# Mixer products in 128x64 halves among a convolution's last step

## The chip, the cores and the metric

The kernel runs on one core of one Trainium2 chip. A core has TensorE (matrix products, with a separate path that loads the stationary operand), VectorE (DVE in the profile), ScalarE (ACT), GpSimd (POOL) and SyncE (SP, which here issues most DMAs). TensorE multiplies a stationary tile of up to 128 rows by 128 columns with a moving operand and writes into PSUM, which has 8 banks; ScalarE and VectorE read the banks and write to the on-chip memory. The metric is the device time of one execution in microseconds; the median of three runs of the kernel before is 226.26 us (226.03 to 226.96).

## The reference

Two branches work on the same input `x = A_q` (2048 tokens, 640 channels) and are mixed by a gate per token:

```python
g = _sigmoid((x * gate_w).sum(-1, keepdims=True))
return g * a + (1 - g) * b
```

Branch `a` is a long convolution. The key is shifted by a short filter of four taps and multiplied with the value (`kv`); `kv` is convolved over the 2048 tokens with a kernel of the same length per channel, by an FFT of 4096; the result is multiplied by the query. Branch `b` is a Mixer block:

```python
h = _gelu(_layernorm(x) @ w1)                 # 640 -> 640
hs = concat(four channel groups of h, shifted by 1, -1, 2, -2 tokens) @ w2
x1 = x + hs
h2 = _gelu(_layernorm(x1) @ w3) @ w4          # 640 -> 1536 -> 640
return x1 + h2
```

## The kernel before

Everything is written as a list of 778 tasks (`build`). A task has an engine, a function that issues its instructions, the tasks it depends on, and the buffers it takes and gives back. The order of all tasks is a string of numbers written out by hand (`ORDER`); a letter behind a number chooses the engine where there are two. `place` walks through that order once with a model of the times and picks for every task its buffer numbers: above all the PSUM banks (`U`). Its model adds `SWITCH` (0.096) to a TensorE task whose `mode` differs from that of the task before, so the label `mode` can influence which bank a task gets; it changes no instruction by itself. Then every engine's instructions are issued in that order, and the framework adds the waits.

The 2048 tokens are 16 blocks of 128 (`s`), four blocks make a quarter (`c`). The Mixer's second half does this for each quarter: layer norm and a transpose by DMA give `x1nT`; twelve tasks `w3.c.fb` (line 810 on) each multiply five tiles of W3 with the quarter's 512 tokens into one bank, five matmuls of 128x128 with 512 columns; ScalarE takes the GELU of each bank (line 820) into `h2T`. Then for each block a task `w4.s` (line 827) multiplies twelve tiles of `h2T` with W4, 512 columns and then 128 columns, 24 matmuls in two banks, and VectorE adds the result to `x` (line 842). For blocks 12 to 15 (`LATE`) w4 is two tasks of twelve matmuls, `w4.s.0` with 512 columns and `w4.s.1` with 128 (line 834), each in a bank of its own.

The convolution is four steps of small products around transfers through DRAM. Steps 1 to 3 use tiles of 64 and 32 rows. Step 4 (line 1023) makes the output of one block: a product with 64 stationary columns for each half of the output partitions, with 512 and with 128 columns of the moving operand. So a task `s4.s` has four matmuls on 128x64 tiles: the two halves of 512 columns, then the two of 128. It needs a load of `GX` from DRAM. VectorE then multiplies its two banks with the gate and the query (`yq`, line 1029; the query arrives by a DMA into `QO`, two buffers for pairs of blocks), and adds the Mixer's part (`ad`, line 1056, or for blocks 12 to 15 `ax`, line 1037, and after w4 `fo`, line 1043). The output is stored by SyncE, for blocks 12 to 15 by SyncE and ScalarE.

In the last part of the order TensorE's tasks stand like this (`s4` is the convolution's last step, the rest the Mixer's):

```
... w4.9 w4.6 | s4.6 s4.7 | w3.3.0 w3.3.6 | s4.2 s4.3 | w3.3.1 w3.3.3 | s4.4 s4.5 s4.1 | w4.8 w3.3.4 w3.3.11 |
s4.0 s4.9 s4.8 | w3.3.7 w3.3.5 w3.3.8 w3.3.2 w3.3.9 | s4.15 | w3.3.10 | s4.10 s4.14 s4.11 | w4.13.0 w4.12.0 |
s4.12 s4.13 | w4.13.1 w4.14.0 w4.12.1 w4.14.1 w4.15.0 w4.15.1
```

A bar marks a change between 128x128 and 128x64 tiles. VectorE's order in the same stretch puts `yq` of blocks 15 and 14 with their `ax`, then `ad` and `yq` of blocks 0, 1, 11, 10, 13, 12, and last the eight `fo` of blocks 12 to 15, of which block 15's two end the work.

Of the kernel before, what the change touches and what calls it, by code (L numbers as in the profile page):

```python
# [16 lines left out]
P = 128  # L17
# [17 lines left out]


ORDER = """
41 0 23 5 29 94v 6 7 9 3 19 11 17 4 25 1 2 31 32 15 18 8 10 63v 12 13 14 26 27 87v 61a 85a 64 62 95v 104v 65v 28
42 88 86 393 24 44 96 209 43 210 55a 66v 89v 67 395 56 68a 58a 53v 54 97v 34 90a 30 399 396v 400v 57v 91 397 40
394a 93a 98 59 99v 100v 92v 60v 101 103v 143 147 16 20p 33 149 398a 102a 77a 145 79v 21 45 150 80 391 71v 72 46  # L40
22 144 148 69v 392v 82v 74a 121 39 122 450 70 78 146 107a 73v 458 35 75 451v 401p 438 37 81v 76v 439a 151 83
113v 123 36 459a 38 456 152 457a 49 84v 108 114 454 452 115v 116 125 455a 453a 110v 129 117v 446 444 126 460
118v 403 404 405 124 127 447a 162 163 406 130 128 156 157 440 105a 441a 407 159 153 154 106 160 461 47 445a 402
131 158 109a 155 442 111 132 137 443a 112a 408 161 462 466 48 138 409 463a 448 134 135 468 215p 216 449 164 140
469a 467a 119 413 141 51 221p 165 470 410 50 411 120a 166 222 223v 464 465a 167 474 471a 173 475a 174 171 217a
480 168 476 187 191 481a 482 193 477a 172 473 192 188 412 414 218 483a 478 169 195 189 170 181 415 416 417 479a
472 418 419 421 422 182 178 179 485 196 194 190 486 423 488 219a 484 225a 489a 175 220 487a 492 176 493a 136 203
424 204 494 425 490 206 498 207 495a 200 201 491a 420 426 427 428 430 502 499a 226 177 504 224 505a 211 503a 506
500 227 496 501a 239 507a 133 497 228 240 508 142 429 184 185 139 247 431 432 433 434 435 436 248 233 510 512
511a 231 513a 243 259p 509 249 514 235 234 260 232 244 515a 518 245 265p 250 236 229 52 519a 516 437 212 246  # L50
517a 520 241 242 237 230 522 266 261v 523v 526 238 530 527a 197 524 531a 528 255 521 529a 269v 262 525v 186 694v
263a 180 205 208 532 267v 303v 198 253 251 257 256 533 183 268 309v 353v 213 202 310 254 270 252 304 313a 264
307v 199 311v 534 535 537 271 539 258 536v 305a 538a 354 540 541v 272 571 566 542 555 293 544 543a 545 572 294
574 575a 289 567 569 570v 573a 550 290 277 598 556 558 278 568v 291 551 557a 292 552a 306 559v 553 546 554a 547a
279 280 283 576 577 284 548v 603 604 606 607a 599 587 287 635 312 273 600a 288 560 561 562 274 285 564a 605v 601
355v 308 286 563v 588 589a 590 591a 602v 582 275 276 578 314 614 580a 619 608 583 609 347p 348 579a 315 325 316
667 584v 549 585 357v 586a 214 615 617 335 616v 620 326 622 336 623a 592 618a 317 323 318 324 621v 593 610 611a
630 612v 333 636 334 631 633 329 349v 662 319 637v 624 634a 646 706 632a 625 594 281 330 320 647 595a 596v 648v
724 638 282 651 649 581 351v 321 565 652 597 639a 654 350 653a 650v 655a 331 626 322 656 657 628a 295 640 641
668 332 670 627a 669a 337 613 678 338 296 642 671v 643v 644a 683 658 663 352 660a 664a 327 328 358 665 659v 679  # L60
695 666a 356 672 673 681 343 684 661 682a 680a 685a 344 674 686 687a 688 629 297 645 675a 689 676v 690 677 301
692v 691a 693 345 302 341 298 299 723 725 346 342 300 696 728 359 371 705 707 729 710 714 360 372 361 365 362
# [4 lines left out]
"""  # L67
ENGINE = {"a": "ACT", "v": "DVE", "p": "POOL"}

# [286 lines left out]
def build(env, nc, io):  # L356
# [6 lines left out]
    ONE = ("U", 1, False)  # L363
# [50 lines left out]
    def c_ones(t):  # L414
# [6 lines left out]
        w=[("K", "z")], roles=("K",))  # L421

    def c_warm(t):
# [4 lines left out]
        r=["WA"], w=["WB"])  # L428
# [354 lines left out]
    def f_st2(t, s0):  # L783
# [3 lines left out]
        nc.gpsimd.tensor_tensor(out=nb, in0=r, in1=SS("S1")[:, c], op=ALU.mult)  # L787
        nc.gpsimd.tensor_scalar(out=nb, in0=nb, scalar1=-1.0 / D, scalar2=None, op0=ALU.mult)

    LATE, late = (12, 13, 14, 15), {}  # L790
    for c in range(4):
        nT, nP = None, f"x1nT{c % 2}"
        for s0 in (4 * c, 4 * c + 2):
            ss = (s0, s0 + 1)
            add(f"ve2.{s0}", {"DVE": 0.42, "POOL": 1.5}, 0, lambda t, s0=s0: f_ve2(t, s0), r=[("x", s, 0) for s in ss] + [("S2", s) for s in ss],
                w=[("v2", s0)])
            add(f"st2.{s0}", "POOL", 1.5, lambda t, s0=s0: f_st2(t, s0), r=[("v2", s0)] + [("x", s, 0) for s in ss],
                w=[("r2", s) for s in ss])
            for s in ss:
                def f_nm2(t, s=s):  # L800
                    k = slice(s, s + 1)
                    norm(t, env["xn"][:, t.buf["xn"][0], :], env["x"][:, s, :], SS("r2")[:, k], SS("SB")[:, k])
                n = add(f"nm2.{s}", {"DVE": 0.445, "ACT": 0.93}, 0, f_nm2, r=[("r2", s), ("x", s, 0)], acq=("xn",))
                def f_dt(t, s=s, n=n, nP=nP):
                    nc.sync.dma_start_transpose(out=env.nT(int(nP[-1]))[:, s % 4, :, :], in_=env["xn"][:, n.buf["xn"][0], :])
                tt = add(f"dt2.{s}", "SP", 1.25, f_dt, use=[n] + ([nT] if nT else []), rel=[(n, "xn")], nbytes=P * D * BF * 1.8,
                         acq=() if nT else (nP,), w=[("x1nT", s)], after=("hsT",) if c % 2 else ())
                nT = nT or tt
        h2 = None
        for fb in range(12):  # L810
            def w3(t, fb=fb, nP=nP):
                for kb in range(5):
                    nc.tensor.matmul(env.PS[:, t.buf["U"][0], :], lhsT=env["W3"][:, kb, 128 * fb:128 * fb + 128],  # L813
                                     rhs=env.nT(int(nP[-1]))[:, :, kb, :], start=(kb == 0), stop=(kb == 4))
            t = add(f"w3.{c}.{fb}", "PE", 1.09, w3, r=["W3"] + [("x1nT", 4 * c + i) for i in range(4)], rel=[(nT, nP)],
                    use=[h2] if h2 else [], acq=[ONE] if h2 else [ONE, "h2"], after=("xnT",), mode="f")
            h2 = h2 or t

            def g2(t_, fb=fb, t=t, o=h2):
                nc.scalar.activation(out=env["h2T"][:, o.buf["h2"][0], fb, :], in_=env.PS[:, t.buf["U"][0], :], func=ACT.Gelu_apprx_tanh)  # L820
            add(f"g2.{c}.{fb}", "ACT", 0.61, g2, use=[t], rel=[(t, "U")], w=[("h2", c, fb)])
        for s in range(4 * c, 4 * c + 4):
            def w4(t, s=s, o=h2):
                m = env.Uf(t.buf["U"][0])
                for (c0, c1) in ((0, 512), (512, 640)):
                    for fb in range(12):
                        nc.tensor.matmul(m[:, c0:c1], lhsT=env["h2T"][:, o.buf["h2"][0], fb, 128 * (s % 4):128 * (s % 4) + 128],  # L827
                                         rhs=env["W4"][:, fb, c0:c1], start=(fb == 0), stop=(fb == 11))
            kw = dict(r=["W4"] + [("h2", c, fb) for fb in range(12)], rel=[(h2, "h2")], mode="f")
            if s in LATE:  # L830
                for n, (c0, c1) in enumerate(((0, 512), (512, 640))):
                    def w4n(t, c0=c0, c1=c1, s=s, o=h2):
                        for fb in range(12):
                            nc.tensor.matmul(env.PS[:, t.buf["U"][0], 0:c1 - c0], lhsT=env["h2T"][:, o.buf["h2"][0], fb, 128 * (s % 4):128 * (s % 4) + 128],  # L834
                                             rhs=env["W4"][:, fb, c0:c1], start=(fb == 0), stop=(fb == 11))
                    late[s, n] = add(f"w4.{s}.{n}", "PE", (2.62, 0.68)[n], w4n, acq=[ONE], **kw)
                continue
            t = add(f"w4.{s}", "PE", 3.28, w4, acq=("U",), **kw)

            def t2(t_, s=s, t=t):  # L840
                x = env["x"][:, s, :]
                nc.vector.tensor_tensor(out=x, in0=env.Uf(t.buf["U"][0])[:, 0:D], in1=x, op=ALU.add)  # L842
            add(f"t2.{s}", "DVE", 0.83, t2, use=[t], rel=[(t, "U")], w=[("x", s, 0), ("x", s, 1)])
# [255 lines left out]
```

## Time and profile before

| | |
|---|---|
| median of three runs | 226.26 us |
| profiled execution, first to last instruction | 225.3 us |
| TensorE busy | 214.4 us (95%) |
| VectorE busy | 188.8 us (84%) |
| ScalarE busy | 154.7 us (69%) |
| GpSimd busy | 45.9 us (20%) |

The profile gives the profiled execution's span from first to last instruction, 225.3 us; the time of a run also holds what lies around it, and the median is 0.96 us above the span. In the views, PE is TensorE, PEld its weight loads, which overlap its matmuls; L followed by a number is a line of the kernel; a name such as `PS<-W,h2T` gives the tile that an instruction writes and those that it reads; `128*64` is the size of the stationary tile, `128x512` that of the moving operand. In the chain of waits, each row is a piece of the chain of work that ended last: when the piece begins, how long it is, and whose work it is. Records of some matmuls can be missing, and matmuls overlap each other's ends, so the start to start distance tells more than a record's length.

### The profile page before, as it was taken

How to read it: one execution, taken by the hardware profiler on the slowest of the kernel's cores; microseconds unless marked ns; L12 is line 12 of the kernel's file. 1: busy time of each engine (PE TensorE's matmuls, PEld its weight loads, DVE VectorE, ACT ScalarE, POOL GpSimd, SP SyncE). 2: the span in 40 equal slices, each digit the busy share in tenths (PEclk: the TensorE clock that was granted, in tenths of full speed). 3: DMA queues.
4: the chain of work that ended last, by engine and by line, in shares of the span. 5: the costliest groups of instructions: out<-in, count | busy, mean ns of one | idle time of the engine just before them, and what ended most of it. 6: DMA issues, size and time to landing. Idle time of an engine off the chain costs nothing.

```text
span 225.3 us, 5017 instructions
## 1 busy us (share of the span) xinstructions
PE 214.4 (95%) x1978; PEld 104.2 (46%) x1998; DVE 188.8 (84%) x281; ACT 154.7 (69%) x225; POOL 45.9 (20%) x86
## 2 busy tenths in 40 slices
PE   3999999999999999999999999999999999999993
PEld 1576454556444444345543333334445554544462
DVE  7898897999999999997479989899767327988993
ACT  6988999699988999789568988878875002125000
POOL 7373451446100009920800000000000000000000
PEclk9999999999999999999999999999999999999998
DMA  6999998999999969979999969999982596888524
GB/s 194 274 335 244 238 245 255 292 225 355 322 210 368 205 231 298 378 254 246 237 390 311 305 190 288 279 323 340 221 269 87 160 414 188 256 268 249 166 58 116
DMA packets 39501, 57.90 MB, mean 257 GB/s; under 512 B 15027, under 2 KB 30645, under 8 KB 39478
## 3 DMA queue, kind: packets, MB, share of 16 engines
q1 hardware_dynamic: 39158, 57.27, 88.9%
q10 hardware_dynamic: 320, 0.33, 0.5%
q8 instruction: 15, 0.25, 0.4%
q14 instruction: 8, 0.07, 0.1%
HBM read 35.56 MB, written 18.36 MB: 239 GB/s over the span
## 4 chain that ended last, share of the span: by engine, by line
PE 72%; DVE 11%; DMA 9%; ACT 4%; issue 2%; POOL 1%; DVEq 0%; POOLq 0%
PE PS L813 18%; PE PS L827 17%; PE PS L716 9%; DMA C<-TRIG 7%; PE PS L834 6%; PE PS L957 5%; PE PS L690 4%; PE PS L985 4%; DVE VC L870 3%; DVE VC L874 3%; PE PS L1023 2%; DMA K<-in_A_k_dram 2%; ACT FS L388 2%; PE PS L256 2%; PE PS L903 2%
## 5 line engine op out<-in xcount | busy, mean ns | idle before, releaser
L820 ACT ACTIVATE h2T<-PS 128x512 bf16<-128x512 f32 x48 | 27.9, 605 | 28.4 <-PE PS L813 28.0
L827 PE MATMUL PS<-W,h2T 128*128 128x128 bf16 (+1 forms) x281 | 39.8, 297 | 0.4
L388 ACT CAST FS<-PS 128x1024 bf16<-128x1024 f32 x37 | 36.0, 1019 | 5.6 <-PE PS L905 3.5
L813 PEld LDWEIGHTS <-W 128*128 128x128 bf16 x240 | 21.1, 98 | 30.7 <-issue 9.4
L827 PEld LDWEIGHTS <-h2T 128*128 128x128 bf16 x288 | 22.2, 98 | 18.9 <-issue 1.9
L388 ACT CAST XH<-PS 128x1024 bf16<-128x1024 f32 x26 | 25.5, 1020 | 7.5 <-PE PS L957 7.4
L813 PE MATMUL PS<-x1nT,W 128*128 128x512 bf16 x120 | 28.5, 380 | 0.0
L813 PE MATMUL PS<-XB,W 128*128 128x512 bf16 x120 | 28.5, 380 | 0.0
L972 DVE TENSOR_TENSOR PP<-XH 128x2048 bf16<-128x2048 bf16 x20 | 23.7, 1220 | 3.1 <-ACT XH L388 2.8
L870 DVE TENSOR_TENSOR VC<-K,VC 128x2560 bf16<-128x2560 bf16 x16 | 23.7, 1491 | 1.7 <-DMA W<-in_B_w_dram 1.5
L716 PE MATMUL PS<-W,hsT 128*128 128x128 bf16 (+1 forms) x155 | 23.5, 297 | 1.0 <-ACT hsT L707 0.7
L842 DVE TENSOR_TENSOR x<-PS,x 128x640 bf16<-128x640 f32 x12 | 9.8, 824 | 13.7 <-PE PS L827 13.7
L690 PE MATMUL PS<-xnT,W 128*128 128x512 bf16 x80 | 19.2, 379 | 0.1
L716 PEld LDWEIGHTS <-hsT 128*128 128x128 bf16 x160 | 12.8, 98 | 13.1 <-DMA W<-in_B_w_dram 1.2
L874 DVE TENSOR_TENSOR VC<-VC 128x2560 bf16<-128x2560 bf16 x12 | 17.9, 1491 | 0.3
L390 DVE CAST XH<-PS 128x1024 bf16<-128x1024 f32 x14 | 16.9, 1220 | 1.2 <-PE PS L957 1.1
L1029 DVE SCALAR_TENSOR_TENSOR W<-PS,GG,QO 128x640 bf16<-128x640 f32 x16 | 13.6, 879 | 2.5 <-PE PS L1023 2.2
L388 ACT CAST GS<-PS 128x1024 bf16<-128x1024 f32 x12 | 12.0, 1016 | 3.9 <-PE PS L985 3.9
L256 PE MATMUL PS<-C 128*128 128x512 bf16 x34 | 10.7, 460 | 3.8 <-DVE C L507 3.7
L834 PE MATMUL PS<-W,h2T 128*128 128x128 bf16 (+1 forms) x94 | 13.3, 298 | 0.1
L723 DVE SCALAR_TENSOR_TENSOR x<-PS,x 128x640 bf16<-128x640 f32 x16 | 12.9, 820 | 0.3 <-PE PS L716 0.3
L957 PE MATMUL PS<-FX,TRIG 64*32 64x512 bf16 x320 | 12.4, 381 | 0.3 <-ACT GS L388 0.3
(115 smaller groups left out, 292.5 us busy)
## 6 DMA issues: line engine op xcount, KB each, us to landing
FH<-FS SPq DMA_DIRECT2D x8, 640.0 KB, 5.3
FXD<-FS SPq DMA_DIRECT2D x8, 640.0 KB, 5.4
FX<-FH SPq DMA_DIRECT2D x10, 512.0 KB, 5.8
FX<-FXD SPq DMA_DIRECT2D x10, 512.0 KB, 5.3
GX<-GD SPq DMA_DIRECT2D x8, 640.0 KB, 5.9
W<-in_B_w_dram SPq DMA_DIRECT2D x2, 1920.0 KB, 11.9
GD<-GS SPq DMA_DIRECT2D x8, 480.0 KB, 4.4
SK<-in_A_ssm_k_dram SPq DMA_DIRECT2D x5, 512.0 KB, 6.8
```

Of the source, the lines that this page charges most:

```text
L388: nc.scalar.copy(out=out, in_=in_)
L390: (nc.vector if t.on == "DVE" else nc.gpsimd).tensor_copy(out=out, in_=in_)
L690: nc.tensor.matmul(m[:, b, :], lhsT=W[:, 0, kb, 160 * fb:160 * fb + 128], rhs=rhs(kb, shifts[fb]), start=(kb == 0), stop=(kb == 4))
L716: nc.tensor.matmul(m[:, c0:c1], lhsT=env["hsT"][:, o.buf["hs"][0], fb, 128 * (s % 4):128 * (s % 4) + 128], rhs=env["W12"][:, 1, fb, c0:c1] ...
L813: nc.tensor.matmul(env.PS[:, t.buf["U"][0], :], lhsT=env["W3"][:, kb, 128 * fb:128 * fb + 128], rhs=env.nT(int(nP[-1]))[:, :, kb, :], star ...
L820: nc.scalar.activation(out=env["h2T"][:, o.buf["h2"][0], fb, :], in_=env.PS[:, t.buf["U"][0], :], func=ACT.Gelu_apprx_tanh)
L827: nc.tensor.matmul(m[:, c0:c1], lhsT=env["h2T"][:, o.buf["h2"][0], fb, 128 * (s % 4):128 * (s % 4) + 128], rhs=env["W4"][:, fb, c0:c1], st ...
L834: nc.tensor.matmul(env.PS[:, t.buf["U"][0], 0:c1 - c0], lhsT=env["h2T"][:, o.buf["h2"][0], fb, 128 * (s % 4):128 * (s % 4) + 128], rhs=env ...
L870: nc.vector.tensor_tensor(out=VC[:, o], in0=env["K"][:, a + 3 - j:a + 7 - j, :], in1=w, op=ALU.mult)
L874: nc.vector.tensor_tensor(out=VC[:, 1], in0=VC[:, 1], in1=VC[:, 2], op=ALU.add)
L957: nc.tensor.matmul(env.U(t.buf["U"][0])[32 * j:32 * j + 32, gp, :], lhsT=CRI()[64 * gp:64 * gp + 64, 32 * pc:32 * pc + 32], rhs=X[64 * gp: ...
L972: nc.vector.tensor_tensor(out=env["PP"][:, o.buf["PP"][0], a, :].rearrange("p (b c) -> p b c", b=2), in0=X.unsqueeze(1).broadcast_to([P, 2 ...
```

## The change

The Mixer's products from the first step-4 task on are issued as pairs: instead of one matmul with a stationary tile of 128x128, two with 128x64, one for each half of the output partitions. Both halves read the same moving operand, and the second follows the first at once. This holds for w3 of the last quarter (`c == 3`), for w4 of block 8 and for w4 of blocks 12 to 15, whose tasks get the mode `c64` that the step-4 tasks have. The numbers in `ORDER` are the same, only broken into other lines.

```diff
+    def halves_of(t):
+        return ((0, 64), (64, 64)) if t.mode == "c64" else ((0, P),)
+
     LATE, late = (12, 13, 14, 15), {}
+    COLS = (8, 12, 13, 14, 15)
...
             def w3(t, fb=fb, nP=nP):
                 for kb in range(5):
-                    nc.tensor.matmul(env.PS[:, t.buf["U"][0], :], lhsT=env["W3"][:, kb, 128 * fb:128 * fb + 128],
-                                     rhs=env.nT(int(nP[-1]))[:, :, kb, :], start=(kb == 0), stop=(kb == 4))
+                    for q, w in halves_of(t):
+                        nc.tensor.matmul(env.PS[q:q + w, t.buf["U"][0], :], lhsT=env["W3"][:, kb, 128 * fb + q:128 * fb + q + w],
+                                         rhs=env.nT(int(nP[-1]))[:, :, kb, :], start=(kb == 0), stop=(kb == 4))
             t = add(f"w3.{c}.{fb}", "PE", 1.09, w3, r=["W3"] + [("x1nT", 4 * c + i) for i in range(4)], rel=[(nT, nP)],
-                    use=[h2] if h2 else [], acq=[ONE] if h2 else [ONE, "h2"], after=("xnT",), mode="f")
+                    use=[h2] if h2 else [], acq=[ONE] if h2 else [ONE, "h2"], after=("xnT",), mode="c64" if c == 3 else "f")
...
                 for (c0, c1) in ((0, 512), (512, 640)):
                     for fb in range(12):
-                        nc.tensor.matmul(m[:, c0:c1], lhsT=env["h2T"][:, o.buf["h2"][0], fb, 128 * (s % 4):128 * (s % 4) + 128],
-                                         rhs=env["W4"][:, fb, c0:c1], start=(fb == 0), stop=(fb == 11))
-            kw = dict(r=["W4"] + [("h2", c, fb) for fb in range(12)], rel=[(h2, "h2")], mode="f")
+                        for q, w in halves_of(t):
+                            a = 128 * (s % 4) + q
+                            nc.tensor.matmul(m[q:q + w, c0:c1], lhsT=env["h2T"][:, o.buf["h2"][0], fb, a:a + w],
+                                             rhs=env["W4"][:, fb, c0:c1], start=(fb == 0), stop=(fb == 11))
+            kw = dict(r=["W4"] + [("h2", c, fb) for fb in range(12)], rel=[(h2, "h2")], mode="c64" if s in COLS else "f")
             if s in LATE:
...
                         for fb in range(12):
-                            nc.tensor.matmul(env.PS[:, t.buf["U"][0], 0:c1 - c0], lhsT=env["h2T"][:, o.buf["h2"][0], fb, 128 * (s % 4):128 * (s % 4) + 128],
-                                             rhs=env["W4"][:, fb, c0:c1], start=(fb == 0), stop=(fb == 11))
+                            for q, w in halves_of(t):
+                                a = 128 * (s % 4) + q
+                                nc.tensor.matmul(env.PS[q:q + w, t.buf["U"][0], 0:c1 - c0], lhsT=env["h2T"][:, o.buf["h2"][0], fb, a:a + w],
+                                                 rhs=env["W4"][:, fb, c0:c1], start=(fb == 0), stop=(fb == 11))
```

More of the change, by code (lines that the diff above doesn't have):

```diff
@@ L37 @@
 ORDER = """
[L38 to L62, printed above, removed]
[4 rows of a table removed]
+41 0 23 5 29 94v 6 7 9 3 19 11 17 4 25 1 2 31 32 15 18 8 10 63v 12 13 14 26 27 87v 61a 85a 64 62 95v 104v 65v 28 42 88
@@ new lines @@
+86 393 24 44 96 209 43 210 55a 66v 89v 67 395 56 68a 58a 53v 54 97v 34 90a 30 399 396v 400v 57v 91 397 40 394a 93a 98
+59 99v 100v 92v 60v 101 103v 143 147 16 20p 33 149 398a 102a 77a 145 79v 21 45 150 80 391 71v 72 46 22 144 148 69v
+392v 82v 74a 121 39 122 450 70 78 146 107a 73v 458 35 75 451v 401p 438 37 81v 76v 439a 151 83 113v 123 36 459a 38 456
+152 457a 49 84v 108 114 454 452 115v 116 125 455a 453a 110v 129 117v 446 444 126 460 118v 403 404 405 124 127 447a 162
+163 406 130 128 156 157 440 105a 441a 407 159 153 154 106 160 461 47 445a 402 131 158 109a 155 442 111 132 137 443a
@@ new lines @@
+112a 408 161 462 466 48 138 409 463a 448 134 135 468 215p 216 449 164 140 469a 467a 119 413 141 51 221p 165 470 410 50
+411 120a 166 222 223v 464 465a 167 474 471a 173 475a 174 171 217a 480 168 476 187 191 481a 482 193 477a 172 473 192
+188 412 414 218 483a 478 169 195 189 170 181 415 416 417 479a 472 418 419 421 422 182 178 179 485 196 194 190 486 423
+488 219a 484 225a 489a 175 220 487a 492 176 493a 136 203 424 204 494 425 490 206 498 207 495a 200 201 491a 420 426 427
+428 430 502 499a 226 177 504 224 505a 211 503a 506 500 227 496 501a 239 507a 133 497 228 240 508 142 429 184 185 139
@@ new lines @@
+247 431 432 433 434 435 436 248 233 510 512 511a 231 513a 243 259p 509 249 514 235 234 260 232 244 515a 518 245 265p
+250 236 229 52 519a 516 437 212 246 517a 520 241 242 237 230 522 266 261v 523v 526 238 530 527a 197 524 531a 528 255
+521 529a 269v 262 525v 186 694v 263a 180 205 208 532 267v 303v 198 253 251 257 256 533 183 268 309v 353v 213 202 310
+254 270 252 304 313a 264 307v 199 311v 534 535 537 271 539 258 536v 305a 538a 354 540 541v 272 571 566 542 555 293 544
+543a 545 572 294 574 575a 289 567 569 570v 573a 550 290 277 598 556 558 278 568v 291 551 557a 292 552a 306 559v 553
@@ new lines @@
+546 554a 547a 279 280 283 576 577 284 548v 603 604 606 607a 599 587 287 635 312 273 600a 288 560 561 562 274 285 564a
+605v 601 355v 308 286 563v 588 589a 590 591a 602v 582 275 276 578 314 614 580a 619 608 583 609 347p 348 579a 315 325
+316 667 584v 549 585 357v 586a 214 615 617 335 616v 620 326 622 336 623a 592 618a 317 323 318 324 621v 593 610 611a
+630 612v 333 636 334 631 633 329 349v 662 319 637v 624 634a 646 706 632a 625 594 281 330 320 647 595a 596v 648v 724
+638 282 651 649 581 351v 321 565 652 597 639a 654 350 653a 650v 655a 331 626 322 656 657 628a 295 640 641 668 332 670
@@ L67 @@
+627a 669a 337 613 678 338 296 642 671v 643v 644a 683 658 663 352 660a 664a 327 328 358 665 659v 679 695 666a 356 672
+673 681 343 684 661 682a 680a 685a 344 674 686 687a 688 629 297 645 675a 689 676v 690 677 301 692v 691a 693 345 302
[5 rows of a table added]
 """
```

9 rows, old and new, of the table ORDER are left out of this document.

## Prediction

> **What bounds the kernel now.** I read the page first, then the sums by stretch for the last 35 us, then the chain of waits there, and last the timelines of TensorE and VectorE for the same stretch. The page, and the sums of the last of those stretches:
>
> ```profile
> span 225.3 us, 5017 instructions
> PE 214.4 (95%) x1978; PEld 104.2 (46%) x1998; DVE 188.8 (84%) x281; ACT 154.7 (69%) x225; POOL 45.9 (20%) x86
> ...
> L820 ACT ACTIVATE h2T<-PS 128x512 bf16<-128x512 f32 x48 | 27.9, 605 | 28.4 <-PE PS L813 28.0
> ```
> ```profile
> core 0: us, PE busy (x) PEld busy (x) DVE busy (x) ACT busy (x) POOL busy (x), PEclk, DMA share, GB/s
> 207.50:221.50 14.00, 13.89 (x106) 7.61 (x104) 13.39 (x19) 0.00 (x0) 0.00 (x0) 1.00 0.45 130
> ```
>
> TensorE is busy 95% of the span and 13.89 of the last 14.00 us, at the full granted clock (1.00). VectorE is close behind: 13.39 of the last 14.00 us. So TensorE sets the end, and VectorE is the engine that takes over if TensorE gets faster. The chain of waits (start, length, what) from the convolution's last step (line 1023) to the end:
>
> ```profile
> 186.34 0.66 PE PS L1023 x8
> 187.00 2.27 PE PS L813 x10
> 189.26 0.66 PE PS L1023 x8
> 189.93 2.27 PE PS L813 x10
> 192.19 0.94 PE PS L1023 x12
> 193.13 0.32 PE PS L827
> 193.45 0.05 issue
> 193.50 2.99 PE PS L827 x22
> 196.50 2.16 PE PS L813 x10
> 198.65 0.94 PE PS L1023 x12
> 199.59 5.50 PE PS L813 x25
> 205.09 0.39 PE PS L1023 x4
> 205.49 1.19 PE PS L813 x5
> 206.67 0.94 PE PS L1023 x12
> 207.61 0.32 PE PS L834
> 207.93 0.05 issue
> 207.98 4.91 PE PS L834 x22
> 212.89 0.66 PE PS L1023 x8
> 213.56 2.29 PE PS L834 x19
> ...
> 220.89 1.02 DVE QO L1043 x2
> ```
>
> Lines 813, 827 and 834 are the Mixer's products (128x128 tiles), line 1023 the convolution's (128x64 tiles). The pieces join without a wait for anything but TensorE itself; the "issue" rows stand where a matmul's record is missing. So each time the tile shape changes shows as an excess of a piece over its matmuls.
>
> **The price of a matmul and of a change of shape.** Line 813 at 196.50 follows another 128x128 product: 10 matmuls of 512 columns in 2.16 us, 0.216 each. For 128 columns I take this row of TensorE's timeline (the last matmul's record is 0.22 long): (0.67 - 0.22) / 8 = 0.056 each.
>
> ```profile
> 216.81 0.67 PE L834 MATMUL PS<-W,h2T 128*128 128x128 bf16 x9
> ```
>
> A product of line 1023 is one pair of 128x64 halves with 512 columns and one pair with 128. Its pieces of 4, 8 and 12 matmuls take 0.39, 0.66 and 0.94, so one more product costs 0.27 to 0.28, and 0.216 + 0.056 = 0.272 is inside that: a pair of halves takes the time of one full matmul. What is left over is the entry: 0.39 - 0.272 = 0.118, 0.66 - 0.544 = 0.116, 0.94 - 0.816 = 0.124.
>
> The way back, at each of seven places, by the same sum: 187.00: 2.27 - 2.16 = 0.11; 189.93: 0.11; 193.13 with its two following rows: 3.36 - (12 x 0.216 + 12 x 0.056 = 3.264) = 0.10; 199.59: 5.50 - 25 x 0.216 = 0.10; 205.49: 1.19 - 1.08 = 0.11; 207.61 with the next two: 5.28 - 24 x 0.216 = 0.10; 213.56: 2.29 - (12 x 0.056 + 7 x 0.216 = 2.184) = 0.11. Sum 0.74.
>
> **The change part by part.** From 186.34 to the end of TensorE's work all products are then 128x64 tiles: w3 of the last quarter (line 813), w4 of block 8 (827), w4 of blocks 12 to 15 (834), and the step-4 products, already so. No other task stands between them in the order. So:
> - All seven ways back go: -0.74 us.
> - Of seven entries the first stays, because the product before it (w4 of block 6) keeps 128x128 tiles. The other six go: 0.116 + 0.124 + 0.124 + 0.118 + 0.124 + 0.116 = -0.72 us.
> - 180 matmuls become pairs: 60 of w3, 24 of block 8, 96 of blocks 12 to 15; 120 have 512 columns, 60 have 128. At the price above a pair costs what its matmul cost: 0. Bounds: the step from 0.39 to 0.94 can be read as 0.270 to 0.280 per two pairs, so -1 to +4 ns per pair, -0.2 to +0.7 us over 180. I take 0, since 0.272 fits all seven pieces. The bound above that is the rival on weight loads.
> - 360 more instructions go through TensorE's queue. A run of 128-column pairs asks for one matmul each 28 ns, for 48 in a row where blocks 12 and 14 follow each other. The next row has 64 starts in 1.93 - 0.37 = 1.56 us, 24 ns each, so this pace was kept for longer. I cost it at nothing; the cover is the filled queue.
>
> ```profile
> 159.16 1.93 PE L985 MATMUL PS<-PP,TRIG 32*64 32x512 bf16 x64
> ```
>
> - DMAs, their order and the other engines' instructions stay. The planner counts a change of shape in its own times and picks PSUM banks by them, so a bank may differ. The chain shows no wait for a bank now, so a better choice gains nothing; a worse one waits for part of a read, at most VectorE's 0.88 us (below). I take 0, as the rows are nearest to that.
>
> TensorE's sum: -1.46 us.
>
> **Who is late next.** VectorE's timeline (start, length, what, idle before and its releaser):
>
> ```profile
> 197.64 0.88 DVE L1029 SCALAR_TENSOR_TENSOR W<-PS,GG,QO 128x640 bf16<-128x640 f32 x1 [0.21 <-DMA QO<-in_A_q_dram]
> 199.09 0.88 DVE L1029 SCALAR_TENSOR_TENSOR W<-PS,GG,QO 128x640 bf16<-128x640 f32 x1 [0.57 <-PE PS L1023]
> ...
> 205.53 0.88 DVE L1029 SCALAR_TENSOR_TENSOR W<-PS,GG,QO 128x640 bf16<-128x640 f32 x1 [0.66 <-PE PS L1023]
> 206.45 0.89 DVE L1037 SCALAR_TENSOR_TENSOR W<-x,OG,W 128x640 bf16<-128x640 bf16 x1
> 207.45 0.88 DVE L1029 SCALAR_TENSOR_TENSOR W<-PS,GG,QO 128x640 bf16<-128x640 f32 x1
> ...
> 220.89 1.02 DVE L1043 SCALAR_TENSOR_TENSOR QO<-PS,OG,W 128x512 bf16<-128x512 f32 x2 [0.43 <-PE PS L834]
> ```
>
> From 205.53 VectorE runs with no idle, in the rows left out neither, until it waits 0.43 us for the last block. The start at 205.53 waits for step 4 of block 15, the piece at 205.09. Ahead of it lie four ways back (0.11 + 0.11 + 0.10 + 0.10) and four entries that go (0.116 + 0.124 + 0.124 + 0.118, its own among them): 0.90 us earlier. VectorE's own work before it allows that: its 0.66 us of idle and the 0.6 us by which the start at 199.09 moves. A little is won at 207.45, which now also waits for TensorE: it begins 0.11 after the end of 206.45's instruction, which itself begins 0.04 after the one before, so 0.07. VectorE is then ready for the last block 0.90 + 0.07 = 0.97 earlier, and with the 0.43 it can follow TensorE by 1.40 of the 1.46 us. The very last instruction (128 columns) needs TensorE's last product and not VectorE's pace, so the two are level.
>
> One new wait is likely. The start at 197.64 waited for a load of q (0.21 idle), and step 4 of block 8 needs the PSUM pair that it frees at 198.52. That product is the third of a group whose first matmul starts at 198.58:
>
> ```profile
> 198.58 1.01 PE L1023 MATMUL PS<-GX,BT 128*64 128x512 bf16 x12
> ```
>
> It starts at 198.58 + 0.30 + 0.27 = 199.15 now and would start 0.68 earlier (three ways back, three entries), at 198.47. If the load comes as late as before, that is a wait of 0.05 us and the way of a release, 0.1 together. The last GELU (0.605 by the page's row) stays covered: only the eleventh matmul of the next product reads it, 10 x 0.216 = 2.16 us after that product's first.
>
> The sum: 1.40 - 0.05 (half of that wait) = 1.35 us. The profiled execution's span goes from 225.3 to 223.9; with the 0.96 us by which the median of the runs, 226.26, stands above the span, 224.9 us. That is -0.6%; this measurement can tell about 0.5%, 1.13 us, from no change.
>
> **A rule that speaks against it.** Records of weight loads, min/median/max in ns:
>
> ```profile
> L1023 PEld LDWEIGHTS <-BT x64: 106/110/110, 186.3 to 213.1; 128*64 128x64 bf16 x64
> L813 PEld LDWEIGHTS <-W x135: 95/98/99, 130.4 to 206.1; 128*128 128x128 bf16 x135
> ```
>
> Half a tile takes no less to load than a whole one, 110 against 98 ns. Both are longer than the 56 ns of a 128-column matmul that hides them, and in line 1023 one 128-column pair does hide the loads of the next pair. The Trainium skill, "TensorEngine Tiling (Array Packing)", section "Restrictions and Gotchas", says that column tiling switches off the fast weight load, and "TensorE: Matmul & The Clock Gate", section "LDWEIGHTS", prices a load by its columns, 64 / 1.2 = 53 ns: an estimate from that page is 53 ns per pair if both halves load at once, which fits under 56 ns, and 107 if one follows the other, 51 ns more on each of 60 pairs, 3.1 us. By that, the time would be 226.26 - 1.46 + 3.1 = 227.9. The trace agrees with the first reading for pairs that alternate 512 and 128 columns, and shows no 128-column pair behind another.
>
> **The rivals.**
> - Slower: weight loads of halves set the pace of the 60 pairs of 128 columns, in w4 of block 8 and in the second parts of blocks 12 to 15. Price, by the load's record: 110 - 56 = 54 ns each, 3.24 us; 226.26 - 1.46 + 3.24 = 228.0. It takes the gain away from 24 ns a pair (1.46 / 60) and shows as slower from 43 ns. For it: the longer record, and that the trace has no run of such pairs. Against it: 0.272 for a product whose 128-column pair has to hide two half loads. Chance 0.13.
> - Within 0.5%: VectorE takes the place. If a late load of q or a changed bank holds its start at 205.53 where it is, the last block follows after 0.43 + 0.07 = 0.50 us of gain: 225.8. The gain shows only if that start moves by 0.63 us or more (1.13 - 0.50). For it: 13.39 of 14.00 us busy, and a load of q that is late already (0.21 at 197.64). Against it: 0.66 us of idle in front. Chance 0.19, a pair price of 2 to 8 ns included (226.0 to 226.2 at its end).
> - The change doesn't do what it says: halves run one after the other. 120 x 0.216 + 60 x 0.056 = 29.3 us more, 254. The 0.272 of line 1023 excludes it nearly: 0.01.
>
> **How the numbers follow.** Forecast 0.67: 224.9, its own range 224.6 to 225.1 (1.66 us of gain with pairs 1 ns cheaper than a matmul, 1.13 us at the other end, where the second case begins). Same 0.19, slower 0.13 + 0.01 = 0.14. The range goes from 224.6 through the second case to 226.2, and leaves out the slow rival.
>
> **What would show it.** Right: line 813 in groups of 20 matmuls at 2.16 us without 0.1 more, entries of 0.12 only at the first piece of line 1023, 128-column pairs 56 ns apart, VectorE's start of 205.53 near 204.6 and its idle before the last block near 0. Wrong: pairs of 128 columns more than 80 ns apart; a wait of TensorE for VectorE between 198 and 208; an end set by VectorE with TensorE done early.

## The result, and the profile after

The changed kernel takes 225.32 us (median, 224.48 to 227.64) against 226.62 us of the kernel before, timed beside it (225.70 to 231.02). The ratio is 0.9951, with a 95% interval of 0.9930 to 0.9973: 1.11 us faster, 0.6 to 1.6 us by the interval. The ratio compares the fast executions of both kernels and not the two medians, which lie 1.30 us apart. The forecast was 224.9 us, 1.35 us below the time before.

The page of the changed kernel, its first lines:

```profile
span 225.3 us, 5381 instructions
## 1 busy us (share of the span) xinstructions
PE 212.7 (94%) x2161; PEld 106.4 (47%) x2178; DVE 189.3 (84%) x281; ACT 154.4 (69%) x225; POOL 45.8 (20%) x86
```

The span is that of the kernel before, 225.3 us. This execution is one of the longer ones of the changed kernel (its time was 227.05 us), and the reason lies ahead of the change: the first matmul of step 4 starts at 187.08 us, against 186.27, and up to there the two kernels hold the same instructions. Between executions that start moves by more than the change is worth, so the readings below count from it.

The chain of waits from step 4 on (start, length, what); line 1031 is step 4, 817 w3, 833 w4 of block 8:

```profile
187.15 0.66 PE PS L1031 x8
187.81 2.16 PE PS L817 x20
189.97 0.54 PE PS L1031 x8
190.51 2.16 PE PS L817 x20
192.67 0.81 PE PS L1031 x12
193.49 3.26 PE PS L833 x48
196.75 2.16 PE PS L817 x20
198.90 0.81 PE PS L1031 x12
199.72 5.39 PE PS L817 x50
205.11 0.27 PE PS L1031 x4
205.39 1.10 PE PS L817 x10
...
208.06 0.50 SPq L382
208.56 0.37 issue
208.93 5.50 DMA QO<-in_A_q_dram
...
214.55 0.89 DVE W L1037
```

Two things are to be seen. The excesses are gone: 10 pairs of w3 take 2.16 us where 10 matmuls took 2.27, one step-4 product takes 0.27 where it took 0.39, 24 pairs of block 8 take 3.26 where they took 3.36; only the first piece keeps its 0.66. And the chain leaves TensorE after 206: from there it runs through a load of q (two transfers, issued from 208.06 on, in at 214.43) and VectorE. Before, it stayed on TensorE up to 220.87.

The end of TensorE's timeline, the six tasks of w4 (twelve matmuls or pairs each) that follow the last step-4 product, in the kernel before, where one of the 72 records is missing, and in the changed one:

```profile
213.49 8.03 PE L834 MATMUL PS<-W,h2T 128*128 128x128 bf16 x71
```
```profile
212.84 8.03 PE L842 MATMUL PS<-W,h2T 128*64 128x128 bf16 x144
```

Twice the matmuls in the same 8.03 us: a pair costs what its matmul did. Among them is the case that the kernel before did not have, 128-column pairs one behind another. Eleven of them in a row (the last record is 0.22 long):

```profile
216.60 0.78 PE L842 MATMUL PS<-W,h2T 128*64 128x128 bf16 x22
```

The pairs start (0.78 - 0.22) / 10 = 0.056 us apart, as single matmuls of 128 columns did before. TensorE's stretch, from the first matmul of step 4 to the end of its last, is 213.49 + 8.03 - 186.27 = 35.25 us before and 212.84 + 8.03 - 187.08 = 33.79 us after, 1.46 us less, which is the sum of the prediction. VectorE's start that was at 205.53 also moves as forecast: it comes 205.43 - 187.08 = 18.35 us after the first step-4 matmul, against 19.26 before, 0.91 us earlier. From there on, however, VectorE did not follow all the way (start, length, what, idle before and its releaser):

```profile
205.43 0.88 DVE L1037 SCALAR_TENSOR_TENSOR W<-PS,GG,QO 128x640 bf16<-128x640 f32 x1 [0.44 <-PE PS L1031]
...
212.39 1.68 DVE L1064 SCALAR_TENSOR_TENSOR QO<-x,OG,W 128x640 bf16<-128x640 bf16 x2 [0.26 <-DMA out_dram<-QO]
214.55 0.88 DVE L1037 SCALAR_TENSOR_TENSOR W<-PS,GG,QO 128x640 bf16<-128x640 f32 x1 [0.48 <-DMA QO<-in_A_q_dram]
...
218.16 3.76 DVE L1051 SCALAR_TENSOR_TENSOR QO<-PS,OG,W 128x512 bf16<-128x512 f32 x8
```

Before, it ran from 205.53 without idle and then waited 0.43 us for TensorE. Now it waits for a store that must free its output buffer (0.26) and for a load of q (0.48), and does all eight instructions of the last blocks in one run of 3.76 us, behind TensorE: it ends at 221.92, 1.05 us after TensorE's last matmul (220.87) instead of 0.39.

### The profile page after: what moved, and what is told of

Same layout as the page of the kernel before. It is cut to its first block, busy times and chain, and to the rows that moved or that the text cites. A ratio compares the mean times of both kernels' runs of the same rounds, so it can differ in the third digit from the quotient of the medians.

```text
span 225.3 us, 5381 instructions
## 1 busy us (share of the span) xinstructions
PE 212.7 (94%) x2161; PEld 106.4 (47%) x2178; DVE 189.3 (84%) x281; ACT 154.4 (69%) x225; POOL 45.8 (20%) x86
## 4 chain that ended last, share of the span: by engine, by line
PE 63%; DMA 17%; DVE 12%; SPq 3%; issue 2%; ACT 1%; DVEq 0%
PE PS L817 18%; PE PS L833 17%; PE PS L715 9%; DMA x<-in_A_q_dram 7%; PE PS L965 5%; DMA W<-in_B_w_dram 4%; PE PS L689 4%; PE PS L993 4%; DMA SK<-in_A_ssm_k_dram 3%; DVE VC L878 3%; DVE VC L882 3%; DMA QO<-in_A_q_dram 2%; SPq L382 2%; PE PS L911 2%; PE PS L1031 1%
## 5 line engine op out<-in xcount | busy, mean ns | idle before, releaser
L833 PE MATMUL PS<-W,h2T 128*128 128x512 bf16 (+3 forms) x306 | 39.8, 298 | 0.3
L817 PEld LDWEIGHTS <-W 128*128 128x128 bf16 (+1 forms) x300 | 22.1, 103 | 29.4 <-issue 8.4
L833 PEld LDWEIGHTS <-h2T 128*128 128x128 bf16 (+1 forms) x312 | 22.4, 100 | 18.5 <-issue 1.6
L817 PE MATMUL PS<-XB,W 128*64 128x512 bf16 (+1 forms) x180 | 28.5, 380 | 0.0
L255 PE MATMUL PS<-C 128*128 128x512 bf16 x34 | 9.9, 434 | 3.8 <-DVE C L506 3.7
L842 PE MATMUL PS<-W,h2T 128*64 128x512 bf16 (+1 forms) x192 | 13.4, 299 | 0.0
```

What stands on the lines that cost most here:

```text
L817: nc.tensor.matmul(env.PS[q:q + w, t.buf["U"][0], :], lhsT=env["W3"][:, kb, 128 * fb + q:128 * fb + q + w], rhs=env.nT(int(nP[-1]))[:, :, ...
L833: nc.tensor.matmul(m[q:q + w, c0:c1], lhsT=env["h2T"][:, o.buf["h2"][0], fb, a:a + w], rhs=env["W4"][:, fb, c0:c1], start=(fb == 0), stop= ...
```

## The experiments

Theory: a change of tile shape costs TensorE 0.12 us on the way to 128x64 and 0.10 to 0.11 us on the way back, a pair costs nothing more than its matmul, and what is missing of 1.46 us is VectorE's wait for DMAs. Rivals: the planner's labels (through its times and banks), pairs as such, a price of a pair that eats part of the gain, and chance. For each kernel below, the stretch of TensorE, how long after TensorE's last matmul VectorE ends, and the time from the first step-4 matmul to the end of the span, all read from its timelines (before rounding). Each ratio is to the kernel before as timed beside it:

| kernel | first step-4 matmul at, us | TensorE's stretch, us | VectorE ends after, us | step 4 to end, us | ratio to the kernel before (95%) |
|---|---|---|---|---|---|
| before | 186.27 | 35.26 | 0.39 | 39.0 | 1 |
| changed | 187.08 | 33.79 | 1.05 | 38.2 | 0.9951 (0.9930 to 0.9973) |
| again | 185.96 | 33.98 | 0.61 | 38.0 | 0.9934 (0.9902 to 0.9967) |
| again_2 | 185.70 | 33.79 | 0.43 | 37.6 | 0.9940 (0.9916 to 0.9964) |
| labels_only | 187.17 | 35.26 | 0.39 | 39.0 | 0.9984 (0.9952 to 1.0015) |
| w3_only | 186.20 | 34.35 | 0.39 | 38.1 | 0.9968 (0.9942 to 0.9994) |
| all_pairs | 185.39 | 33.76 | 0.40 | 37.5 | 0.9958 (0.9935 to 0.9981) |
| three_q | 188.16 | 33.79 | 0.40 | 37.55 | 0.9945 (0.9913 to 0.9976) |
| three_q_2 | 188.21 | 33.79 | 0.54 | 37.7 | 0.9944 (0.9916 to 0.9972) |
| before_three_q | 187.26 | 35.26 | 0.39 | 39.0 | 0.9977 (0.9949 to 1.0005) |

**The labels without the pairs.**

```diff
     def halves_of(t):
-        return ((0, 64), (64, 64)) if t.mode == "c64" else ((0, P),)
+        return ((0, P),)
```

> The tasks carry the new mode labels, so the planner's times and banks are those of the changed kernel, but every Mixer product is one matmul on a 128x128 tile as before. Theory that the changes of shape are the gain: the stretch stays at 35.25 us, ratio 1.000 (0.998 to 1.002). Rival that the planner's labels gave it: ratio 0.995.

The stretch is 35.26 us and the chain has its excesses back:

```profile
187.24 0.66 PE PS L1031 x8
187.90 2.27 PE PS L817 x10
190.16 0.66 PE PS L1031 x8
190.83 2.27 PE PS L817 x10
193.09 0.94 PE PS L1031 x12
194.03 3.37 PE PS L833 x24
```

The ratio holds 1 in its interval; 0.995 lies only just outside, so the stretch says more than the time. The labels gave nothing. Listing what the planner picks for both kernels says why: engines and banks are the same for all 778 tasks.

**A part of the pairs.**

```diff
-            kw = dict(..., mode="c64" if s in COLS else "f")
+            kw = dict(..., mode="f")
```

> Only w3 of the last quarter in pairs; w4 of blocks 8 and 12 to 15 as 128x128 tiles. Then three entries into 128x64 and three ways back are left in the stretch of seven and seven, so by the price of a change (0.12 in, 0.10 to 0.11 back) four of each go: 4 x 0.12 + 4 x 0.105 = 0.90 us, and the stretch from the first matmul of step 4 to TensorE's last takes 34.36 us. Rival that the gain comes from issuing pairs as such, 1.47 us over 180 pairs, 8 ns each: 60 pairs give 0.49 us, 34.77 us. Ratio 0.996 by the first, 0.998 by the second.

The stretch is 34.35 us, against 34.36 by the count of changes and 34.77 by the count of pairs. The excesses stand exactly where a shape still changes (w4 of block 8 between step 4 and w3, w4 of blocks 13 and 12 behind step 4, step 4 behind them) and nowhere else:

```profile
191.80 0.81 PE PS L1031 x12
192.61 3.37 PE PS L833 x24
195.98 2.28 PE PS L817 x20
198.26 0.81 PE PS L1031 x12
...
206.63 5.29 PE PS L842 x24
211.92 0.66 PE PS L1031 x8
```

24 matmuls of block 8 come out at 3.37 instead of 3.26 (way back), the pairs of w3 behind them at 2.28 instead of 2.16 (entry), step 4 at 211.92 at 0.66 instead of 0.54 (entry). With 14 changes of shape in the kernel before, 6 here and 1 in the changed kernel, the count explains three stretches to 0.01 us. That shows the changes of shape to be the gain. The time alone could not: 0.9968 with 0.9942 to 0.9994 holds both 0.996 and 0.998.

**Pairs everywhere.**

```diff
-                    ..., mode="c64" if c == 3 else "f")
+                    ..., mode="c64")
...
-            kw = dict(..., mode="c64" if s in COLS else "f")
+            kw = dict(..., mode="c64")
```

> All of w3 and w4 in pairs, in every quarter and block: 444 pairs more than the changed kernel. Most of these products stand beside 128x128 tiles or beside the 32 and 64 row tiles of steps 1 to 3, where a change of shape happens either way; of the listed changes 85 are left against 84. If a pair costs what its matmul cost, the time is that of the changed kernel (ratio 0.994 to 0.996) and w3 outside the stretch takes 1.08 us for 5 pairs with no change of shape beside them. If a pair costs 4 ns more, the upper end of the bound, 1.8 us are added: ratio 1.002. If half loads set the pace of 128-column pairs (54 ns), 132 such pairs more add 7 us.

The ratio is that of the changed kernel, and its interval excludes 1.002 and the 7 us. Ahead of step 4, w3 stands between products of other tile shapes. TensorE's timeline there, of the kernel before (one and two tasks in a group), then of this one:

```profile
121.20 1.25 PE L813 MATMUL PS<-XB,W 128*128 128x512 bf16 x5
122.38 0.63 PE L957 MATMUL PS<-FX,TRIG 64*32 64x512 bf16 x16
123.13 1.07 PE L985 MATMUL PS<-PP,TRIG 32*64 32x512 bf16 x32
124.14 2.33 PE L813 MATMUL PS<-XB,W 128*128 128x512 bf16 x10
```
```profile
120.13 1.27 PE L817 MATMUL PS<-XB,W 128*64 128x512 bf16 x10
121.33 0.63 PE L965 MATMUL PS<-FX,TRIG 64*32 64x512 bf16 x16
122.09 1.07 PE L993 MATMUL PS<-PP,TRIG 32*64 32x512 bf16 x32
123.09 2.35 PE L817 MATMUL PS<-XB,W 128*64 128x512 bf16 x20
```

One task takes 1.27 against 1.25 and two tasks 2.35 against 2.33: 0.02 more for a group, not for a pair. The second five pairs cost 2.35 - 1.27 = 1.08 us, as the five matmuls do. So pairs win only where the neighbour has their shape, and cost 0.02 us per group where it has a third one, here 64x32 or 32x64.

**Three buffers for the loads of q.** The two free slots of the tile `QO` become a third buffer, in the changed kernel and in the kernel before.

```diff
-                    ("GX", 4), ("Q", 2), ("O", 2), ("V", 4)):
+                    ("GX", 4), ("Q", 3), ("O", 2), ("V", 4)):
...
-        qown = halves(..., lambda t, g: env["QO"][64 * g:64 * g + 64, 2 * t.buf["Q"][0]:2 * t.buf["Q"][0] + 2, :],
+        qown = halves(..., lambda t, g: env["QO"][64 * g:64 * g + 64, (0, 2, 8)[t.buf["Q"][0]]:(0, 2, 8)[t.buf["Q"][0]] + 2, :],
...
-                                               in1=env["QO"][:, 2 * q.buf["Q"][0] + i, :], op0=ALU.mult, op1=ALU.mult)
+                                               in1=env["QO"][:, (0, 2, 8)[q.buf["Q"][0]] + i, :], op0=ALU.mult, op1=ALU.mult)
```

> The changed kernel with three buffers instead of two for the loads of q (two free slots of the same tile), so the load for blocks 12 and 13 waits for an older reader and can be issued some 1.7 us earlier. Theory that a late load of q holds back VectorE's tail and with it part of TensorE's gain: VectorE has no idle for a load after 205, the last block follows TensorE, ratio 0.9935 to 0.994, that is 0.2 to 0.4 us below the changed kernel. Rival that VectorE's own instructions or chance set it: the same as the changed kernel within 0.1 us.

> The kernel before with three buffers for the loads of q and nothing else. TensorE sets its end, VectorE waits 0.43 us for the last block, so an earlier load is hidden: ratio 1.000 (0.998 to 1.002), stretch 35.25 us. If the loads cost time in the kernel before too, 0.997.

> Three buffers for q once more: VectorE ends 0.4 us after TensorE, from the first matmul of step 4 to the end 37.55 us (the changed kernel 37.96 to 38.19, the kernel before 38.99). If that reaches the time, the ratio is 0.992 to 0.994, below the changed kernel beside it; if the loads of q that now go out earlier disturb the work ahead of step 4, that work ends later and the ratio is that of the changed kernel or above.

In three_q the chain stays on TensorE to the end, and VectorE waits for no DMA. The end of its chain, and VectorE's rows where the two waits were:

```profile
213.54 0.54 PE PS L1031 x8
214.09 7.21 PE PS L842 x120
221.30 0.02 issue
221.32 1.02 DVE QO L1051 x2
```
```profile
213.25 1.68 DVE L1064 SCALAR_TENSOR_TENSOR QO<-x,OG,W 128x640 bf16<-128x640 bf16 x2
214.84 0.88 DVE L1037 SCALAR_TENSOR_TENSOR W<-PS,GG,QO 128x640 bf16<-128x640 f32 x1
```

From step 4 to the end it takes 37.55 us, 1.45 us less than the kernel before: nearly the whole of TensorE's gain. In three_q_2, the same kernel, another load of q is late, the one for blocks 8 and 9:

```profile
203.53 1.68 DVE L1037 SCALAR_TENSOR_TENSOR W<-PS,GG,QO 128x640 bf16<-128x640 f32 x2 [0.71 <-DMA QO<-in_A_q_dram]
```

VectorE then runs to the end without a wait and ends 0.54 us after TensorE, 37.7 us from step 4 to the end, where 0.4 and 37.55 were expected. In the kernel before the same edit changes nothing, 39.0 us (its ratio has both 1 and 0.997 in the interval), and VectorE still waits for TensorE at the end:

```profile
221.88 1.02 DVE L1043 SCALAR_TENSOR_TENSOR QO<-PS,OG,W 128x512 bf16<-128x512 f32 x2 [0.43 <-PE PS L834]
```

So the missing part of the gain was VectorE's wait for DMAs: where no such wait stands in its last stretch, as in three_q and all_pairs, it follows TensorE by nearly all of its gain. That the third buffer takes them away is not shown: all_pairs and again_2, with two buffers, end 0.40 and 0.43 us after TensorE as well, and three_q_2 has a wait of its own. In the times the third buffer doesn't show either: 0.9945 and 0.9944 against 0.9934 and 0.9940 of the changed kernel beside it, with intervals of 0.3% to either side, and the median of three_q_2 is 225.12 against 225.16 us. Two profiles with the third buffer happen to reach step 4 late (188.2), which is ahead of every instruction that the edit moves; whether that is chance is left open. The version is not shown to be better or worse.

**The changed kernel once more.**

> The changed kernel itself, beside the others of this group. From the first matmul of step 4 to TensorE's last matmul the kernel before takes 221.52 - 186.27 = 35.25 us; with 13 changes of shape gone it should take 33.79 us. Time 0.995 of the kernel before. If the load of q that VectorE waited for at 214.55 was late by chance, that wait is absent here and the ratio comes nearer to 0.9935 (1.46 us).

> The changed kernel once more, beside the one with three buffers for q. Stretch 33.8 to 34.0 us; VectorE ends 0.4 us after TensorE if its loads come in time, up to 1.1 us if the load for blocks 12 and 13 comes late; ratio 0.993 to 0.996.

In `again` the other wait is to be seen, the one that the prediction priced. VectorE's row for blocks 1 and 0, then TensorE's for the step-4 products of blocks 0, 9 and 8:

```profile
197.40 1.68 DVE L1037 SCALAR_TENSOR_TENSOR W<-PS,GG,QO 128x640 bf16<-128x640 f32 x2 [0.83 <-DMA QO<-in_A_q_dram]
```
```profile
197.62 1.18 PE L1031 MATMUL PS<-GX,BT 128*64 128x512 bf16 x12
```

The load of q for blocks 0 and 1 came late, VectorE freed the PSUM pair late, and TensorE's group took 1.18 us instead of 0.98: its stretch is 33.98 us. The wait at 214.55 for the load for blocks 12 and 13 is absent, as expected if it was chance, but VectorE waits 0.38 us for a store and ends 0.61 us after TensorE. The ratio of 0.9934 is the one expected for that case, though its interval holds 0.9951 as well. In `again_2` TensorE waits for nothing, VectorE ends 0.43 us after it, and 37.6 us from step 4 to the end are 1.4 us less than before. So the three profiles of the changed kernel keep 0.8, 1.0 and 1.4 us of 1.46.

## Why the prediction was right

- **Prices of a change of shape.** Right to 0.01 us: 33.79 us in two of the three profiles of the changed kernel and 34.35 us with a part of the pairs, as counted from the rows of the kernel before.
- **A pair costs its matmul.** Right, also where the kernel before showed nothing: 128-column pairs one behind another. The bound of +4 ns per pair is excluded by the 8.03 us of w4 and by all_pairs.
- **The rival on weight loads** falls. Weight loads of the changed kernel's w4:

```profile
L842 PEld LDWEIGHTS <-h2T x192: 110/110/110, 207.1 to 220.6; 128*64 128x64 bf16 x192
```

  Each record is still 110 ns long, but pairs of 128 columns keep their 56 ns, so the record's length isn't the pace. By the estimate from the Trainium skill ("TensorE: Matmul & The Clock Gate", section "LDWEIGHTS"), the loads of a pair take 53 ns if both halves load at once and 107 ns if one follows the other. The trace agrees with the first as to the pace: in a run of 128-column pairs the two loads of a pair start 3 to 4 ns apart, and 56 ns a pair excludes 107. For a single load the record's 110 ns stand against the page's 53.
- **360 more instructions at nothing.** TensorE shows no gap for them. The changed kernel's traces do hold instruction fetches at other places than before; see the last section.
- **A late load at the start of 197.64, 0.05 us.** The mechanism was right, the size not: 0, 0.2 and 0 us of TensorE's time in three profiles. The 0.2 us, in `again`, is the wait of TensorE for VectorE that the prediction named as a sign of being wrong.
- **VectorE follows by 1.40 us.** That is the term that was mis-sized. The start at 205.53 moved by 0.91 us, as the step said. But it took VectorE's rows from there on as work without a wait and moved them all earlier. Two of them depend on DMAs that did not end earlier along with them: the load of q for blocks 12 and 13 and the store that frees an output buffer. They took 0.66 us of VectorE's gain in the first profile, 0.22 in the second, 0.04 in the third (VectorE's end after TensorE, less 0.39). In the first profile the end was set by VectorE with TensorE done 1.05 us earlier, another of the prediction's signs of being wrong. The second rival, VectorE in TensorE's place, was thus partly true, with a DMA as its cause, though not at the start that it named.
- **The numbers.** 1.35 us forecast, 1.11 us measured with 0.6 to 1.6 as its interval, 0.49% against the bound of 0.5% on which the chance of "faster" was put: the measurement lies at that bound and decides for neither side. How near the sum came is not shown more closely: from step 4 on, the three profiles keep between 0.8 and 1.4 us. The two groups timed later give 1.5 us (227.09 x 0.0066) and 1.4 us (226.7 x 0.0060). The time of 225.32 us is 0.4 above the forecast, of which 0.36 is the kernel before, timed at 226.62 instead of 226.26. It is outside the forecast's own range (224.6 to 225.1), in the part of the range that the prediction left to the second rival. The 0.96 us between span and time, by which the prediction got its time, set the median of three executions against the span of another: in each of the 21 executions of the changed kernel the time is 1.7 to 1.9 us above its own span. The forecast is 226.26 - 1.35 either way.

## What to carry to other kernels

Where TensorE sets the end and small-tile products stand between large ones, count the changes of tile shape from the chain of waits: each group's length less its matmuls at the steady pace. Splitting the large product into concurrent halves of the small one's shape removed them here at no price per matmul, but only between neighbours that then share a shape. Before counting a shorter engine path as time, follow the DMAs that feed the next engine: moving its instructions earlier is worth only as much as their loads and stores move with them.

## What was not expected of the hardware

- **A change of shape costs in two places.** Part is a gap of some 0.1 us either way. Part is the first weight load, which starts together with its matmul (186.26 and 186.27 us in the kernel before), while those behind it start during the matmul before theirs. Matmul records of the kernel before, min/median/max in ns:

```profile
L1023 PE MATMUL PS<-GX,BT x64: 219/299/403, 186.3 to 213.3; 128*64 128x512 bf16 x32, 128*64 128x128 bf16 x32
L813 PE MATMUL PS<-XB,W x75: 379/379/390, 130.4 to 206.3; 128*128 128x512 bf16 x75
```

  The first matmul behind a change is 403 ns long on a half tile and 390 on a whole one, against 379: 24 and 11 ns. The difference of 13 ns is most of the 0.02 us by which groups of pairs are longer in all_pairs.
- **A load can land later though it is issued earlier.** The load of q for blocks 12 and 13 is two transfers. Counted from the first step-4 matmul, the first was issued at 22.1 us before and at 21.0 to 21.2 us after, and its last part was in at 25.3 us before and at 27.0, 26.1 and 26.0 us in the three profiles after; the second, which VectorE waits for as well, was in 0.4 to 0.5 us later each time. Half of the first transfer's sixteen parts were in at 24.8 us before and at 23.8 to 24.4 after; the last part came 0.5 us behind that before and 1.7 to 2.9 us after. The load of `GX` issued ahead of it lags in the kernel before too (half at 22.3, last part at 24.0 us). The change doesn't always bring the lag: in all_pairs the first transfer was issued at 21.0 us and in at 24.5. A 16 KB fetch of instructions, by its number TensorE's (15 in the kernel before, 17 in the changed one, 20 in all_pairs), lies at 23.0 to 24.6 us in the changed kernel and at 19.1 before, so it may be part of it; all_pairs has none there and no lag, but w3_only has none there either and lags (half at 24.1, last part at 25.8 us). The cause isn't settled; nothing here separated the fetch from the stores in front of the load.
